# One decode step of attention with a gated MLP: wq loaded as 16 rows and then 112 rows, with x between them on SyncE's queue

## The chip, the cores and the metric

The kernel runs on one core of one Trainium2 chip. A core has a matrix engine (TensorE, PE in the profile), VectorE (DVE), ScalarE (ACT), GpSimd (POOL) and SyncE (SP). Data come from the chip's main memory by DMA, into an on-chip memory of 128 partitions. The profile counts 16 DMA engines for the core. SyncE and ScalarE each have a DMA queue of their own here, q1 and q10 in the profile.

The metric is the device time of one execution in microseconds. The kernel before takes 678.52 us, the median of three runs (678.5 to 678.8).

## The reference

Eight sequences (B = 8) each bring one new token of width D = 512. x is normalized once, and two branches use it:

```python
xn = layernorm(x)                       # 8 x 512
q  = xn @ wq                            # 512 x 4096: 32 query heads of 128
# 8 key/value heads, each shared by 4 query heads, 4096 cached positions
scores = einsum("bhqd,bhkd->bhqk", q, k) * 128 ** -0.5
o  = einsum("bhqk,bhkd->bhqd", softmax(scores), v)
s  = o.reshape(8, 4096) @ wo            # 4096 x 512

z  = gelu(xn @ w_in)                    # 512 x 1792, two halves of 896
z2 = layernorm(z[..., 896:])
m  = (z[..., :896] * (w_sp * z2 + b_sp)) @ w_out    # 896 x 512
out = x + s * silu(m)
```

All values are float32. The key and value caches are 134 MB each, so that nearly all of the traffic is the two caches, read once.

## The kernel before, in words

**Memory.** Three buffers, slots A, B and C, each have 128 partitions of 16384 floats (64 KB a partition, 8.39 MB in all). Every large load fills a slot or a part of one, always all 128 partitions, with one contiguous row of main memory for each partition. Slot B first holds wq, slot C first holds the MLP's weights (w_in and w_out, 43 KB a partition), and slot A the first half of head 0's keys. Afterwards the slots go round: for each of the 8 key/value heads the keys come as two halves (four sequences each) into A and B, and the values as two halves into C and B. For the last head the values go into A and B, while wo fills C in seven pieces that get smaller.

**Order of the work.** `Recorder` collects every operation in the order in which the program names it, works out which operation must wait for which (by the regions that they read and write) and then emits one stream of instructions for each engine. Nothing is reordered. A load with a `key` shares the semaphore of its slot; a load without one has a semaphore of its own. The heads' part of TensorE's stream runs as a loop of seven rounds, with the last head written out behind it.

**SyncE's queue.** All large loads are issued by SyncE in program order: wq (line 338), w_mlp (line 341), then keys (line 547) and values (line 553) head by head, and wo (line 558). SyncE waits before a load only until TensorE has finished with what the slot held. The first three loads wait for nothing. The fourth, the second half of head 0's keys into slot B, waits until the Q projection has read wq.

**The start.** x, with two scalars of the MLP appended to each row (8 rows of 576 floats, 18 KB), is loaded in two column halves of 288 by ScalarE (lines 334 and 335). VectorE takes its statistics (lines 387 and 388), GpSimd the power -0.5 (line 390), VectorE normalizes (line 391), and TensorE transposes (line 394) into xnT (line 395). x itself is also spread for the residual at the end (lines 402 to 406). `project_q` (lines 415 to 423) then multiplies xnT by wq from slot B in two halves, `mlp` (from line 431) uses slot C, and the heads follow: scores (line 506), softmax, values (lines 538 to 544).

**The end.** The last pieces of wo are multiplied as they land (line 574), and the result is multiplied by the gate, added to x (lines 630 and 631) and stored (line 632).

Of the kernel before, what the change touches and what calls it, by code (L numbers as in the profile page):

```python
# [16 lines left out]
B, D = 8, 512  # L17
# [13 lines left out]
WO_EARLY = 12  # L31
WO_LATE = [(WO_EARLY, 20), (20, 25), (25, 28), (28, 30), (30, 31), (31, 32)]
FOLDED = 24
FOLD_AT = 29
LOOPED = HKV - 1
X_PARTS = 2
ALIGN = 512
XW = D + 64
E = 2
# [280 lines left out]
def gqa_gmlp_decode(real, x, kT, v, wq, wo, w_mlp, out):  # L320
    nc = Recorder(real)

    def sb(name, shape, **kw):
        return real.alloc_sbuf_tensor(name, shape, F32, **kw).ap()
# [4 lines left out]
    slots = {n: sb(f"slot_{n}", [P, SLOT], align_bytes=ALIGN) for n in "ABC"}  # L329
# [1 line left out]
    tbuf = sb("tbuf", [P, B * J * G * REP])  # L331

    xs_sb = pbuf[:B, :XW]
    for c in range(0, XW, XW // X_PARTS):
        nc.scalar.dma_start(xs_sb[:, c:c + XW // X_PARTS], x[:, c:c + XW // X_PARTS])
    x_sb = xs_sb[:, :D]

    nc.sync.dma_start(slots["B"], wq, key="B")
    wq_sb = slots["B"].rearrange("p (k n) -> p k n", k=NK)
    n_in, n_mlp = NK * 2 * FH, NK * 2 * FH + NB * D  # L340
    nc.sync.dma_start(slots["C"][:, :n_mlp], w_mlp, key="C")
# [28 lines left out]
    nc.vector.tensor_copy(same8[:, (E - 1) * B:E * B], same[:, 0, :B])  # L370
    oT_end = sb("oT_end", [P, HKV * REP - FOLDED, (E - 1) * B + R])
    nc.gpsimd.memset(oT_end, 0.0)

    def shift(t, i):
        lo = (E - 1 - i) * B
        return t[:, lo:lo + R]
# [114 lines left out]
    w, wl = sb("w", [P, 1]), sb("wl", [P, 1])  # L491
    oT = sb("oT", [P, FOLDED // REP, REP, B])
    o_all = [sb(f"o_all{i}", [P, G, DH]) for i in range(2)]
# [49 lines left out]
    def combine(b):  # L543
        nc.tensor.matmul(po[:, b * REP:(b + 1) * REP], o_sb[b % 2], fold, start=True, stop=True)  # L544
# [18 lines left out]
    def folded_wo(lo, hi):  # L563
        for m in range(lo, hi):
            h, r = divmod(m, REP)
            nc.tensor.matmul(part[R * r:R * r + B, :], oT[:, h, r, :], wo_sb[:, m, :],
                             start=(m < REP), stop=(m >= FOLDED - REP))

    def direct_wo(lo, hi):
        for m in range(lo, hi):  # L570
            for i in range(E):
                for g in range(G):
                    at = g * P + i * W
                    nc.tensor.matmul(acc[R * g:R * (g + 1), :], shift(oT_end[:, m - FOLDED], i),  # L574
                                     wo_sb[:, m, at:at + W], start=(m == FOLDED and i == 0),
                                     stop=(m == HKV * REP - 1 and i == E - 1))

    def head(h):
# [21 lines left out]
        combine(B - 1)  # L600
        if h < FOLDED // REP:
            to = oT[:, h]
# [17 lines left out]
    nc.vector.tensor_copy(part_sb, part)  # L620
    direct_wo(FOLDED, FOLD_AT)
    for i in range(E):
        for g in range(G):
            lo = g * P + i * W
            nc.tensor.matmul(acc[R * g:R * (g + 1), :], shift(same8, i), part_sb[:, lo:lo + W],
                             start=False, stop=False)
    direct_wo(FOLD_AT, HKV * REP)

# [36 lines left out]
```

## Time and profile before

| | us |
|---|---|
| median of three runs | 678.52 |
| the profiled execution | 678.71 |
| its span, first to last instruction | 677.3 |
| TensorE busy with matmuls | 375.2 |
| VectorE busy | 167.5 |
| ScalarE busy | 13.4 |
| GpSimd busy | 2.8 |

The span is what the profile's views divide up; the execution's own time is 1.4 us longer. The program moved 290.90 MB, which is 429 GB/s over the span. The profile writes a load's duration in two ways: as the short time in which the issuing engine was occupied with issuing it ("SPq" for SyncE's queue, "ACTq" for ScalarE's), and as the time from the issue to its landing, which includes the loads in front of it. In a view by stretches of time a packet is put down, with its whole duration and all its bytes, at its start, so that in stretches of a microsecond the share of the DMA engines can be over 1 or 0 while they are always busy. A packet here is one partition's row of a load, or the short write at the end that reports the load as landed.

### The profile page before, as it was taken

What the parts mean: (1) busy time and instruction counts of PE and PEld (TensorE: products, weight loads), DVE (VectorE), ACT (ScalarE), POOL (GpSimd) and SP (SyncE); (2) the same over time, 40 slices, a digit from 0 to 9 for tenths busy, and PEclk for the clock granted to TensorE, in tenths of its full rate; (3) what the DMA queues carried; (4) which work ended last, traced back from release to release, by engine and by line L of the source; (5) the groups of instructions that cost most, each with busy time, mean ns of one, the idle gap of its engine ahead of it and who ended that gap; (6) DMA issues with size and microseconds to landing.
All of it is one profiled execution on the core that took longest, in us unless ns stands there. A gap on an engine that the chain in (4) does not pass through costs nothing. (4 is left out here: it accounts for less than half of the span.)

```text
span 677.3 us, 5857 instructions
## 1 busy us (share of the span) xinstructions
PE 375.2 (55%) x2658; PEld 119.5 (18%) x2658; DVE 167.5 (25%) x277; ACT 13.4 (2%) x27; POOL 2.8 (0%) x14
## 2 busy tenths in 40 slices
PE   0547554546665455456755454655654465655657
PEld 0122121112111111111211121211211121111212
DVE  2141042302430033401521024401432024400342
ACT  0000000000000000000000000000000000000000
POOL 1000000000000000000000000000000000000000
PEclk9967666878767678877766678887676678766697
DMA  8999999999999999999999999999999999999997
GB/s 373 449 434 434 433 434 433 434 433 433 433 433 433 433 433 433 434 433 433 433 433 433 433 434 433 433 433 437 437 437 437 433 437 445 433 437 434 404 423 318
DMA packets 6233, 290.90 MB, mean 429 GB/s; under 512 B 832, under 2 KB 848, under 8 KB 1360
## 3 DMA queue, kind: packets, MB, share of 16 engines
q1 hardware_dynamic: 6192, 290.75, 99.3%
q8 instruction: 7, 0.11, 0.1%
q10 hardware_dynamic: 32, 0.02, 0.0%
q14 instruction: 2, 0.02, 0.0%
HBM read 290.74 MB, written 0.03 MB: 429 GB/s over the span
## 5 line engine op out<-in xcount | busy, mean ns | idle before, releaser
L506 PE MATMUL sc<-slot_B,qz 128*32 128x512 f32 x512 | 74.4, 746 | 76.6 <-PEq L506 76.6
L538 PE MATMUL o_ps<-slot_B,tbuf 128*16 128x512 f32 x512 | 77.5, 732 | 70.5 <-PEq L538 61.6
L506 PE MATMUL sc<-slot_A,qz 128*32 128x512 f32 x512 | 74.4, 746 | 47.6 <-PEq L506 47.6
L540 DVE TENSOR_TENSOR o_all<-o_ps,diag 128x512 f32<-128x512 f32 x64 | 44.3, 691 | 161.0 <-PE o_ps L538 161.0
L538 PE MATMUL o_ps<-slot_C,tbuf 128*16 128x512 f32 x448 | 67.0, 739 | 20.5 <-PEq L538 20.5
L510 DVE TENSOR_REDUCE nm<-sc 128x1 f32<-128x1024 f32 x8 | 9.8, 1224 | 269.5 <-PE sc L506 269.5
L541 DVE TENSOR_REDUCE o_sb<-o_all 128x128 f32<-128x512 f32 x64 | 67.8, 1060 | 2.2
L506 PEld LDWEIGHTS sc<-slot_B,qz 128*32 128x32 f32 x512 | 20.4, 134 | 130.5 <-issue 130.5
L506 PEld LDWEIGHTS sc<-slot_A,qz 128*32 128x32 f32 x512 | 20.7, 133 | 94.8 <-issue 94.8
L544 PE MATMUL po<-fold,o_sb 128*128 128x4 f32 x128 | 25.6, 270 | 12.3 <-PEq L544 12.3
L544 PEld LDWEIGHTS po<-fold,o_sb 128*128 128x128 f32 x128 | 20.3, 199 | 68.5 <-issue 64.2
L538 PEld LDWEIGHTS o_ps<-slot_B,tbuf 128*16 128x16 f32 x512 | 13.4, 106 | 100.5 <-issue 90.2
L538 PEld LDWEIGHTS o_ps<-slot_C,tbuf 128*16 128x16 f32 x448 | 13.7, 112 | 57.0 <-issue 56.8
L528 PE MATMUL scr<-ident,pbuf 128*128 128x128 f32 x64 | 14.8, 409 | 10.6 <-PEq L528 9.3
L511 ACT ACTIVATE pbuf<-sc,nm 128x1024 f32<-128x1024 f32 x8 | 8.9, 1114 | 556.1 <-DVE nm L510 556.1
L528 PEld LDWEIGHTS scr<-ident,pbuf 128*128 128x128 f32 x64 | 11.8, 211 | 11.0 <-issue 9.7
L529 DVE COPY tbuf<-scr 128x512 f32<-128x512 f32 x16 | 11.1, 692 | 10.6 <-PE scr L528 10.6
L415 PE MATMUL scr<-slot_B,xnT 128*32 128x512 f32 x64 | 9.0, 713 | 8.2 <-PEq L415 8.2
L538 PE MATMUL o_ps<-slot_A,tbuf 128*16 128x512 f32 x64 | 9.8, 753 | 3.9 <-PEq L538 3.9
L514 PE MATMUL scr<-ident,nm 128*1 128x128 f32 x8 | 2.2, 269 | 11.8 <-PEq L514 10.4
L394 PE MATMUL scr<-ident,tbuf 8*128 8x8 f32 x4 | 0.6, 255 | 12.9 <-DVE tbuf L391 12.9
L521 PE MATMUL scr<-wl,same 128*128 128x1 f32 x16 | 3.5, 286 | 6.1 <-PEq L521 5.4
(102 smaller groups left out, 88.4 us busy)
## 6 DMA issues: line engine op xcount, KB each, us to landing
slot_B<-in_v SPq DMA_DIRECT2D x2, 4096.0 KB, 33.8
slot_C<-in_w_mlp SPq DMA_DIRECT2D x1, 5376.0 KB, 34.2
slot_C<-in_wo SPq DMA_DIRECT2D x1, 3072.0 KB, 35.4
slot_C<-in_wo SPq DMA_DIRECT2D x1, 2048.0 KB, 41.4
slot_C<-in_wo SPq DMA_DIRECT2D x1, 1280.0 KB, 44.0
slot_C<-in_wo SPq DMA_DIRECT2D x1, 768.0 KB, 45.4
slot_C<-in_wo SPq DMA_DIRECT2D x1, 512.0 KB, 46.1
slot_C<-in_wo SPq DMA_DIRECT2D x2, 256.0 KB, 46.4
```

What stands on the lines that cost most here:

```text
L415: nc.tensor.matmul(pq[R * g:R * (g + 1), :], xnT[:, k, :], wq_sb[:, k, lo:lo + REP * DH], start=(k == 0), stop=(k == NK - 1))
L506: nc.tensor.matmul(sc[R * g:R * (g + 1), c, :], qz[:, b * R:(b + 1) * R], k_sb[:, i, c, g, :], start=(b == 0), stop=(b == B - 1))
L510: nc.vector.tensor_reduce(nm, sc, op=ALU.max, axis=AX.XY, negate=True)
L511: nc.scalar.activation(p.rearrange("p j s -> p (j s)"), sc.rearrange("p c s -> p (c s)"), AF.Exp, bias=nm, accum_out=l)
L514: nc.tensor.transpose(a, nm, ident)
L521: nc.tensor.matmul(tot, same_all, wl, start=True, stop=True)
L528: nc.tensor.transpose(t[:, j * P:(j + 1) * P], p[:, 4 * c + j, :], ident)
L529: nc.vector.tensor_copy(pT[:, :, 4 * c:4 * c + 4].rearrange("p b j (g r) -> p (j g) b r", g=G), t.rearrange("p (m b r) -> p m b r", b=B, r ...
L538: nc.tensor.matmul(of[R * c:R * c + G * REP, :], pT[:, b, j, :], v_unit[:, j], start=(j < G), stop=(j >= J - G))
L540: nc.vector.tensor_mul(o_all[b % 2], o, diag[:, :, None].to_broadcast([P, G, DH]))
L541: nc.vector.tensor_reduce(o_sb[b % 2], o_all[b % 2].rearrange("p g d -> p d g"), op=ALU.add, axis=AX.X)
L544: nc.tensor.matmul(po[:, b * REP:(b + 1) * REP], o_sb[b % 2], fold, start=True, stop=True)
```

## The change

wq's load is split by rows: partitions 0 to 15 first, then partitions 16 to 127. x is no longer loaded by ScalarE in two halves; SyncE issues it in one transfer between the two parts of wq. The two parts of wq have semaphores of their own, where the whole load had that of slot B, so that the first multiplication with wq waits for both. All other operations are the same and stand in the same order; behind this place their lines are lower by one.

```diff
 FOLDED = 24
+FIRST = 16
 FOLD_AT = 29
 LOOPED = HKV - 1
-X_PARTS = 2
...
     xs_sb = pbuf[:B, :XW]
-    for c in range(0, XW, XW // X_PARTS):
-        nc.scalar.dma_start(xs_sb[:, c:c + XW // X_PARTS], x[:, c:c + XW // X_PARTS])
     x_sb = xs_sb[:, :D]
-
-    nc.sync.dma_start(slots["B"], wq, key="B")
+    nc.sync.dma_start(slots["B"][:FIRST], wq[:FIRST])
+    nc.sync.dma_start(xs_sb, x)
+    nc.sync.dma_start(slots["B"][FIRST:], wq[FIRST:])
     wq_sb = slots["B"].rearrange("p (k n) -> p k n", k=NK)
```

## The prediction

> **What bounds the kernel now.** I read the page's span, slices and queues first, then its chain that ended last, then the start of the timeline and of the DMA traffic, because the change touches only the first three loads.
>
> ```profile
> span 677.3 us, 5857 instructions
> ...
> DMA  8999999999999999999999999999999999999997
> GB/s 373 449 434 434 433 434 433 434 433 433 433 433 433 433 433 433 434 433 433 433 433 433 433 434 433 433 433 437 437 437 437 433 437 445 433 437 434 404 423 318
> ...
> q1 hardware_dynamic: 6192, 290.75, 99.3%
> ...
> q10 hardware_dynamic: 32, 0.02, 0.0%
> ...
> DMA 7%; PE 1%; SPq 0%; DVE 0%; issue 0%
> ```
>
> The transfers are busy in every slice at 433 to 437 GB/s, and SP's queue (q1) takes 99.3% of sixteen engines' span. q10 is ScalarE's queue, which carries only x. The chain is short, and most of it is one wait for a load:
>
> ```profile
> 616.62 8.87 PE sc L506 x64
> ...
> 628.26 46.46 DMA slot_C<-in_wo
> 674.72 0.04 issue
> ```
>
> That load is the last of a queue that never ran dry. Busy time over three stretches (the last two columns are the share of the sixteen DMA engines and GB/s):
>
> ```profile
> 0.00:1.60 1.60, 0.00 (x0) 0.00 (x0) 0.09 (x1) 0.00 (x0) 0.83 (x9) 1.00 0.00 0
> ...
> 40.00:660.00 620.00, 346.54 (x2315) 108.02 (x2308) 155.81 (x242) 12.15 (x26) 0.57 (x1) 0.74 1.00 433
> ```
>
> Nothing moves for 1.6 us, and then the engines are full: share 1.00 at 433 GB/s for 620 us. So the time is the start, plus bytes over rate, plus a tail of some 2.6 us after the last load lands at 674.72. TensorE is busy 346.54 of those 620 us and waits for data. **Whatever the slowest DMA engine loses in the first 40 us is carried to the end**, because later there is no idle DMA time to take it back.
>
> The one place where it could be regained is a stretch in which the queue waits for SP to issue. The page's DMA issues show there is none:
>
> ```profile
> slot_B<-in_kT SPq DMA_DIRECT2D x8, 27.9
> ...
> slot_B<-in_v SPq DMA_DIRECT2D x7, 29.1
> ...
> slot_B<-in_wq SPq DMA_DIRECT2D x1, 21.9
> ```
>
> An 8.39 MB transfer takes 8.39/433 = 19.4 us. The ones into slot B, the latest issued, land 27.9 and 29.1 us after issue, so 8.5 to 9.7 us of other traffic is still ahead of them. A late start shifts their issue as much as their landing, and the margin stays.
>
> **The change part by part.** The start of the kernel:
>
> ```profile
> 0.73 0.90 ACTq L335 DMA_DIRECT2D pbuf<-in_x  x2
> 0.74 0.38 SPq L338 DMA_DIRECT2D slot_B<-in_wq  x1
> 1.16 0.42 SPq L341 DMA_DIRECT2D slot_C<-in_w_mlp  x1
> 1.64 0.42 SPq L547 DMA_DIRECT2D slot_A<-in_kT  x1
> 1.66 1.28 ACT L445 ACT_TABLE_LOAD   x1 [1.66 <-PEq L657]
> 10.55 0.68 DVE L387 BATCH_NORM_STATS2 st<-pbuf 8x6 f32<-8x512 f32 x1 [6.89 <-DMA pbuf<-in_x]
> 13.50 0.19 DVE L395 COPY xnT<-scr 128x32 f32<-128x32 f32 x1 [0.69 <-PE scr L394]
> 22.80 5.35 PE L415 MATMUL scr<-slot_B,xnT 128*32 128x512 f32 x32 [8.25 <-PEq L415]
> 33.25 0.33 SPq L547 DMA_DIRECT2D slot_B<-in_kT  x1
> 43.87 0.63 ACT L445 ACTIVATE pbuf<-pbuf 128x512 f32<-128x512 f32 x1 [40.93 <-DVE pbuf L444]
> ```
>
> *ScalarE's two issues go* (0.90 us). ScalarE's table load can start at about 0.75 instead of 1.66, but its first real work is at 43.87: worth 0. If that cover were gone, it would be worth 0.9 us.
>
> *SP issues three loads where it issued one.* At the 0.38 to 0.42 us of the rows above plus 0.04 between issues, w_mlp and the first K move 2 x 0.46 = 0.9 us later. The engines don't notice: the first 16 rows are 1.05 MB, which is 2.4 us at 433 GB/s, and the third issue is over at about 0.74 + 3 x 0.46 = 2.1 us, before those rows can be through. Cost 0; without that cover up to 0.9 us.
>
> *x lands at another time.* It now stands behind sixteen rows of wq in the same queue. The statistics start at 10.55 and the transposed x is ready at 13.69, so the layernorm needs 3.1 us; its user, the first Q projection, starts at 22.80, when wq has landed. In the changed order x stands ahead of 112 rows, which need at least 112 x 65.5 KB / 433 GB/s = 16.9 us, so x is ready well before wq whatever the sixteen rows cost. Worth 0 either way. That earlier or later layernorm is the visible effect, but not one on the path.
>
> *The projection waits for two loads instead of one.* That is one more wait on TensorE's queue before line 415, which was idle for 8.25 us there: 0.04 us (the "issue" pieces of the chain), hidden because K for slot B is issued with 8.5 us in hand.
>
> *Packets.* Two x transfers of 8 rows with 8 end packets each are the 32 of q10. One x transfer has 16, and one more wq transfer adds 16 end packets: 32 again. 0.
>
> *The two wq transfers themselves.* This is the term that matters. The traffic at the start, put down at the start of each packet:
>
> ```profile
> 1.70:1.90 0.20, 0.00 (x0) 0.00 (x0) 0.17 (x1) 0.20 (x1) 0.20 (x2) 1.00 6.21 1989
> ...
> 2.90:3.00 0.10, 0.00 (x0) 0.00 (x0) 0.10 (x1) 0.04 (x1) 0.00 (x0) 1.00 1.51 655
> ...
> 4.80:5.50 0.70, 0.00 (x0) 0.00 (x0) 0.00 (x0) 0.00 (x0) 0.00 (x0) 1.00 3.46 1498
> ...
> 7.20:7.90 0.70, 0.00 (x0) 0.00 (x0) 0.00 (x0) 0.00 (x0) 0.00 (x0) 1.00 3.49 1511
> ...
> 9.60:10.30 0.70, 0.00 (x0) 0.00 (x0) 0.00 (x0) 0.00 (x0) 0.00 (x0) 1.00 3.46 1498
> ...
> 12.10:12.70 0.60, 0.00 (x0) 0.00 (x0) 0.42 (x1) 0.00 (x0) 0.14 (x1) 1.00 4.03 1748
> ```
>
> In 4.80:5.50 start 1498 x 0.7 = 1049 KB, which is sixteen rows of 65.5 KB: every engine takes one row, and the next sixteen start 2.42 us later (4.8, 7.2, 9.6, 12.1). One engine carries one row in 2.42 us, 27.1 GB/s (2.90:3.00 holds a single row: 1.51 x 0.1 x 16 = 2.42 us). The spread of the starts stays 0.6 to 0.7 us, so in a 128-row transfer no engine gets in another's way. Every large transfer of the kernel has that form, so the trace has no large transfer to fewer partitions, and the price of one is not shown.
>
> The new first transfer lands in 16 neighbouring partitions, and all sixteen engines work there at once. Bounds: if neighbours don't share a way into the memory, one row time, 2.42 us; if all share one, 16 x 2.42 = 38.7 us. Between ends that far apart I take their geometric middle, 9.7 us, in which four rows share a way: the extra over 2.42 is **7.3 us** (0 to 36.3).
>
> [...]
>
> The 112 rows are seven for each engine. Bounds: lined up as the 128 rows are, 7 x 2.42 = 16.9 us, no extra; four to a way all the time, 7 x 9.7 = 67.8 us, 50.9 extra. They cover seven eighths of the partitions, so the nearest row is the 128-row load, which shares nothing; but sevens beginning at row 16 don't line up with a grouping by fours or eights, so neighbouring engines meet for part of the way. I take that the last engine goes at half speed for three of its seven rows: **7.3 us** (0 to 50.9).
>
> *Start.* Sixteen rows may start sooner than 128: the second rows start at 4.8 to 5.5, so the first ones counted from about 2.4 to 3.1, though the first packets are recorded from 1.7. A gain of at most 3.1 - 1.7 = 1.4 us; I take 0, since the first engines to start had no second row earlier than 4.8.
>
> Sum: 7.3 + 7.3 = 14.6 us. The profiled execution took 678.71 us (span 677.3), 0.19 above the median of 678.52; against that median, **693.1 us**, 2.1% slower.
>
> **The rivals.**
>
> *No shared way (not slower).* The sixteen rows cost one row time and the 112 seven. For it: all engines are busy in both transfers, every slice runs at the same 27.1 GB/s per engine, and the bytes are the same. Against it: the trace never has the engines side by side in one region. The time is 678.5, and 677.1 with the whole 1.4 us of the start. It decides from the point where sixteen rows pass in under 3.8 us (2.42 + 1.36, where 1.36 us is 0.2% of the time and about what a measurement of this kernel tells from no change). [...]
>
> *Only the sixteen rows pay.* The seven per engine spread so that no two engines meet. 678.5 + 7.3 = 685.8 us. For it: they cover 112 of 128 partitions; against it: seven divides into no even grouping.
>
> *The 112 rows pay in full.* If the rows are dealt in turn, so that neighbouring rows are in flight together all the time, 678.5 + 7.3 + 50.9 = 736.7 us, or anything from 702 up if the engines drift apart on the way.
>
> **How the numbers follow.** Both loads pay, in part: 0.50, own range 688 to 702. No shared way: 0.21, of which 0.03 gains more than 0.2%. Only the sixteen rows: 0.16. In full: 0.13. The likeliest is 693.1. The range runs from 677.8, to take in most of the not-slower case, to 702, which leaves out the full price (0.13), the larger gains (0.03) and the ends of the rest: about 0.8 inside. Faster 0.04 (the 0.03 and 0.01 for causes not listed), same 0.18, slower 0.78.
>
> **What would show it.** The sharpest mark is the statistics at line 386 of the changed kernel: they start when x lands, about 12.5 to 14 us if the sixteen rows take 9.7, about 6 us if they take 2.42. The second is the first Q projection (line 414): 22.8 if nothing is lost, about 30 if only the sixteen rows pay, about 37 by my sum, past 45 if the 112 rows pay more. The first slice's GB/s falls well below 373, and the later slices stay at 433. The last load of wo lands as much later than 674.72 as the projection starts later than 22.80. The prediction is wrong if x is early and the projection unmoved, or if a late projection is not found again at the end, which would mean a slack in the queue that I read as absent.

## The result and the profile after

The changed kernel takes 699.94 us (median of five runs, 698.69 to 700.33) against 678.68 for the kernel before on the same chip: a ratio of 1.031, with a 95% interval of 1.0295 to 1.0325. That is 21.3 us slower. The profiled execution of the changed kernel has a span of 698.6 us, against 677.3.

The page after, in the lines that answer to those shown of before:

```profile
span 698.6 us, 5856 instructions
...
GB/s 181 240 331 454 425 420 436 454 425 424 428 462 428 420 432 458 424 428 424 447 443 425 428 432 455 424 424 435 454 424 424 432 454 432 424 432 432 429 427 290
...
q1 hardware_dynamic: 6224, 290.77, 99.1%
...
DMA 7%; PE 1%; SPq 0%; DVE 0%; issue 0%
```

Only the first three slices have changed much: 181, 240 and 331 GB/s where there were 373, 449 and 434. The DMA engines still count as busy all the time. They carry the same bytes (290.90 MB on both pages) more slowly. By stretches (the last two columns are the share of the DMA engines and GB/s):

```profile
2.00:12.00 10.00, 0.00 (x0) 0.00 (x0) 1.50 (x8) 0.01 (x1) 0.43 (x3) 1.00 1.07 172
12.00:42.00 30.00, 1.68 (x22) 1.40 (x22) 2.01 (x7) 0.00 (x0) 0.54 (x1) 1.00 0.92 228
42.00:660.00 618.00, 341.05 (x2316) 108.63 (x2320) 148.12 (x241) 12.14 (x26) 0.57 (x1) 0.75 1.00 433
```

From 42 us on, the rate is the 433 GB/s of before. The timeline of the start shows x and wq landing (the statistics wait for x, line 414 for wq):

```profile
0.74 0.38 SPq L335 DMA_DIRECT2D slot_B<-in_wq  x1
1.18 0.36 SPq L336 DMA_DIRECT2D pbuf<-in_x  x1
...
1.58 0.32 SPq L337 DMA_DIRECT2D slot_B<-in_wq  x1
...
12.55 0.68 DVE L386 BATCH_NORM_STATS2 st<-pbuf 8x6 f32<-8x512 f32 x1 [8.89 <-DMA pbuf<-in_x]
...
44.61 5.48 PE L414 MATMUL scr<-slot_B,xnT 128*32 128x512 f32 x32 [28.07 <-issue]
```

x lands 2.0 us later than before and the first Q projection starts 21.8 us later (44.61 against 22.80). The chain that ended last is the old one, moved:

```profile
649.91 46.07 DMA slot_C<-in_wo
695.98 0.04 issue
```

The last piece of wo lands at 695.98, which is 21.3 us later than the 674.72 of before. What the start loses arrives at the end almost whole.

### The profile page after: what moved, and what is told of

It is laid out like the page before. It is cut to its first block, busy times and chain, and to the rows that moved or that the text cites. A ratio compares the mean times of both kernels' runs of the same rounds, so it can differ in the third digit from the quotient of the medians.

```text
span 698.6 us, 5856 instructions
## 1 busy us (share of the span) xinstructions
PE 372.3 (53%) x2658; PEld 119.0 (17%) x2658; DVE 167.4 (24%) x277; ACT 13.4 (2%) x27; POOL 2.8 (0%) x14
## 2 busy tenths in 40 slices
DMA packets 6233, 290.90 MB, mean 416 GB/s; under 512 B 840, under 2 KB 840, under 8 KB 1360
## 5 line engine op out<-in xcount | busy, mean ns | idle before, releaser
L505 PE MATMUL sc<-slot_A,qz 128*32 128x512 f32 x512 | 71.7, 723 | 48.4 <-PEq L505 48.4
L414 PE MATMUL scr<-slot_B,xnT 128*32 128x512 f32 x64 | 9.1, 721 | 28.1 <-issue 28.1
L527 PEld LDWEIGHTS scr<-ident,pbuf 128*128 128x128 f32 x64 | 11.8, 212 | 11.1 <-issue 9.7
L528 DVE COPY tbuf<-scr 128x512 f32<-128x512 f32 x16 | 11.1, 691 | 10.7 <-PE scr L527 10.7
L416 DVE TENSOR_SCALAR pbuf<-scr 128x512 f32<-128x512 f32 x2 | 1.4, 691 | 36.4 <-PE scr L414 36.4
```

The source lines that it names most:

```text
L414: nc.tensor.matmul(pq[R * g:R * (g + 1), :], xnT[:, k, :], wq_sb[:, k, lo:lo + REP * DH], start=(k == 0), stop=(k == NK - 1))
L416: nc.vector.tensor_scalar(q_sb, pq, float(DH) ** -0.5, None, op0=ALU.mult)
L505: nc.tensor.matmul(sc[R * g:R * (g + 1), c, :], qz[:, b * R:(b + 1) * R], k_sb[:, i, c, g, :], start=(b == 0), stop=(b == B - 1))
L527: nc.tensor.transpose(t[:, j * P:(j + 1) * P], p[:, 4 * c + j, :], ident)
L528: nc.vector.tensor_copy(pT[:, :, 4 * c:4 * c + 4].rearrange("p b j (g r) -> p (j g) b r", g=G), t.rearrange("p (m b r) -> p m b r", b=B, r ...
```

## The experiments

### Which part of the change costs the time

Three kernels do one part alone, or the same order with another cut.

*The split alone*, x left on ScalarE's queue:

```diff
+FIRST = 16
...
-    nc.sync.dma_start(slots["B"], wq, key="B")
+    nc.sync.dma_start(slots["B"][:FIRST], wq[:FIRST])
+    nc.sync.dma_start(slots["B"][FIRST:], wq[FIRST:])
```

> wq as 16 rows and then 112 rows, x left on ScalarE's queue in two halves. Theory W (engines that write neighbouring partitions at the same time share a way into the memory) and theory S (the same, but on the side of the source: engines that read neighbouring rows of main memory): the whole loss is in the split, 699 to 700 us, first Q projection at about 44.6. Rival X (the loss comes from x standing in SP's queue between the two parts, so that half of the engines start the 112 rows late): 678.5 us.

Measured: 700.2 us (699.58 to 700.63), ratio 1.0317 (1.03 to 1.0334).

*x alone*, in one transfer on SP's queue, ahead of a whole wq:

```diff
-    for c in range(0, XW, XW // X_PARTS):
-        nc.scalar.dma_start(xs_sb[:, c:c + XW // X_PARTS], x[:, c:c + XW // X_PARTS])
+    nc.sync.dma_start(xs_sb, x)
```

> x in one transfer on SP's queue, ahead of wq, which is whole again. Theories W and S: 678.5 us within 0.5, and x lands at about 4 us instead of 10.55, which is worth nothing because the first Q projection still starts at 22.8 to 23.3. Rival X: slower by several us, since x then delays half of the engines as well.

Measured: 678.98 us (678.72 to 679.27), ratio 1.0005 (0.9996 to 1.0015).

*The same order, cut by columns*: the first 2048 columns of all 128 partitions, x, the other columns (to the changed kernel):

```diff
-FIRST = 16
+FIRST = SLOT // 8
...
-    nc.sync.dma_start(slots["B"][:FIRST], wq[:FIRST])
+    nc.sync.dma_start(slots["B"][:, :FIRST], wq[:, :FIRST])
     nc.sync.dma_start(xs_sb, x)
-    nc.sync.dma_start(slots["B"][FIRST:], wq[FIRST:])
+    nc.sync.dma_start(slots["B"][:, FIRST:], wq[:, FIRST:])
```

> The order of the changed kernel (first part of wq, x, rest of wq, all on SP's queue), but wq is split by columns: 2048 of the 16384 columns for all 128 partitions, then the other 14336. Bytes of the two parts are those of the 16 and 112 rows. Theories W and S: each engine has its own partitions again, 678.5 us within 1, first Q projection at about 23, x lands at about 6 us. Rival F (a split costs by itself: the second transfer starts late, or a transfer of 1 MB runs badly): slower by more than 2 us, the projection late.

Measured: 678.62 us (678.41 to 679.02), ratio 1.0001 (0.9991 to 1.0011). The timelines, first of the split alone:

```profile
22.09 0.68 DVE L389 BATCH_NORM_STATS2 st<-pbuf 8x6 f32<-8x512 f32 x1 [18.43 <-DMA pbuf<-in_x]
44.75 6.14 PE L417 MATMUL scr<-slot_B,xnT 128*32 128x512 f32 x32 [18.66 <-issue]
```

of x alone:

```profile
3.57 0.62 DVE L386 BATCH_NORM_STATS2 st<-pbuf 8x6 f32<-8x512 f32 x1
23.36 6.29 PE L414 MATMUL scr<-slot_B,xnT 128*32 128x512 f32 x32 [15.85 <-PEq L414]
```

and of the cut by columns, where the projection's first eight multiplications start on the first part:

```profile
5.79 0.68 DVE L386 BATCH_NORM_STATS2 st<-pbuf 8x6 f32<-8x512 f32 x1 [2.13 <-DMA pbuf<-in_x]
9.72 1.94 PE L414 MATMUL scr<-slot_B,xnT 128*32 128x512 f32 x8
22.70 5.24 PE L414 MATMUL scr<-slot_B,xnT 128*32 128x512 f32 x24 [11.05 <-DMA slot_B<-in_wq]
```

The whole loss is in the split by rows. x on SP's queue costs and brings nothing that these runs can tell: the time is the same with x landing at 3.57, 5.79 or 10.55 where wq is fast, and nearly the same with 12.55 or 22.09 where wq is slow. Two loads instead of one cost nothing either where each covers all 128 partitions (ratio 1.0001). The columns also size the first term of the sum: the same 1.05 MB ahead of x, in all partitions, let x land at 5.79; in 16 partitions at 12.55. The sixteen rows cost **6.8 us** more, and of the 21.8 us of the projection **15.0** remain for the 112 rows.

### Source or destination

A kernel with twelve loads of wq's rows into slot C ahead of everything, each issued when the one before has landed. Slot C is overwritten afterwards. In this probe and those below, `Recorder` also counts the step between partitions when it works out the region of a load (two lines, left out here).

```diff
+    C = slots["C"]
+    for to, fr in [(C, wq),
+                   (C[0:16], wq[0:16]), (C[0:16], wq[0:128:8]),
+                   (C[0:128:8], wq[0:16]), (C[0:64:4], wq[0:16]), (C[0:112:7], wq[0:16]),
+                   (C[0:4], wq[0:4]), (C[0:16:4], wq[0:4]),
+                   (C[0:32], wq[0:32]), (C[0:64], wq[0:64]),
+                   (C[0:112], wq[0:112]), (C[16:128], wq[16:128])]:
+        nc.sync.dma_start(to, fr)
     nc.sync.dma_start(slots["B"], wq, key="B")
```

> Twelve loads of wq's rows into slot C ahead of everything, each issued when the one before has landed, so that each stands alone: 128 rows; 16 neighbouring rows into 16 neighbouring partitions; every eighth row into 16 neighbouring partitions; 16 neighbouring rows into every eighth partition; the same into every fourth of 64 and every seventh of 112 partitions; 4 rows into 4 neighbouring partitions; 4 rows into every fourth of 16; 32 rows; 64 rows; rows 0 to 111; rows 16 to 127. Slot C is overwritten afterwards by the MLP's weights. With f for the fixed time from issue to landing beyond the data (about 2 us, from the first): theory W, four partitions to a way: 19.4, 9.7, 9.7, 4.8 or less, 4.8 or less, 2.4 to 4.8, 9.7, 2.4, 19.4, 38.7 at most and 19.4 at least, and about 30 for each of the 112-row loads, each plus f. Theory S: 19.4, 9.7, 2.4, 9.7, 9.7, 9.7, plus f: the spread of the source decides and that of the destination doesn't.

Packets by stretches, of the second to the fifth load (each is sixteen rows, 1049 KB):

```profile
24.00:25.50 1.50, 0.00 (x0) 0.00 (x0) 0.00 (x0) 0.00 (x0) 0.00 (x0) 1.00 5.67 699
25.50:35.50 10.00, 0.00 (x0) 0.00 (x0) 0.00 (x0) 0.00 (x0) 0.00 (x0) 1.00 0.00 0
35.50:37.00 1.50, 0.00 (x0) 0.00 (x0) 0.00 (x0) 0.00 (x0) 0.00 (x0) 1.00 5.64 699
37.00:47.50 10.50, 0.00 (x0) 0.00 (x0) 0.00 (x0) 0.00 (x0) 0.00 (x0) 1.00 0.00 0
47.50:49.00 1.50, 0.00 (x0) 0.00 (x0) 0.00 (x0) 0.00 (x0) 0.00 (x0) 1.00 3.11 699
49.00:55.50 6.50, 0.00 (x0) 0.00 (x0) 0.00 (x0) 0.00 (x0) 0.00 (x0) 1.00 0.00 0
55.50:56.50 1.00, 0.00 (x0) 0.00 (x0) 0.00 (x0) 0.00 (x0) 0.00 (x0) 1.00 4.68 1049
```

Sixteen neighbouring rows and every eighth row of the source take the same into the same 16 partitions: the next load begins some 11.5 to 12 us later, both times. With the same sixteen source rows spread over every eighth partition, the next load begins 8 us later. So the destination decides, and theory S falls. Sixteen rows into every seventh partition took 4.1 to 5.1 us a row, where theory W left most of them at 2.4, which led to the next runs.

### Two halves in the kernel

```diff
-FIRST = 16
+FIRST = 64
```

> The changed kernel with wq in two equal parts by rows, 64 and 64, and x between them. The first probe had 64 rows alone at 23.0 us from start to the start of the next, against 22.5 for 128 rows: each half takes nearly as long as the whole. Theory W: wq lands about 20 us later than in one load, the projection starts at about 43 and the time is 697 to 700 us. Rival B (the loss belongs to the small first load and to sevens that line up badly; two halves with four rows for each engine run like the whole): 678.5 to 681 us.

Measured: 699.74 us (699.51 to 699.93), ratio 1.0311 (1.0293 to 1.0328); x lands at 24.00 and the projection starts at 44.20. Theory W holds: what costs isn't a small first load. Equal halves lose as much as 16 and 112.

### What a shared way is

Two kernels in the manner of the first probe, with a small load of all partitions between each two, so that SyncE's issue of that small load marks the landing. Partitions as start, number, step.

```diff
+    C = slots["C"]
+    for lo, n, step in [(0, 8, 4), (64, 8, 4), (4, 8, 4), (0, 8, 8),
+                        (0, 2, 4), (0, 2, 1), (0, 2, 32), (0, 2, 64), (4, 2, 4), (16, 2, 4),
+                        (0, 4, 4), (16, 4, 4), (64, 4, 4), (0, 4, 32),
+                        (0, 16, 7), (0, 96, 1), (0, 128, 1)]:
+        to, fr = C[lo:lo + (n - 1) * step + 1:step], wq[:n]
+        nc.sync.dma_start(to, fr)
+        nc.sync.dma_start(C[:, :128], wq[:, :128])
     nc.sync.dma_start(slots["B"], wq, key="B")
```

> Seventeen loads of wq's rows into slot C, each alone (a load of 128 rows of 512 bytes stands between each two and waits for the one before): partitions given as start, number, step: (0, 8, 4), (64, 8, 4), (4, 8, 4), (0, 8, 8), (0, 2, 4), (0, 2, 1), (0, 2, 32), (0, 2, 64), (4, 2, 4), (16, 2, 4), (0, 4, 4), (16, 4, 4), (64, 4, 4), (0, 4, 32), (0, 16, 7), (0, 96, 1), (0, 128, 1). They ask what a shared way is, since in the first probe 16 rows into every seventh partition took 4.2 to 4.7 us a row although few of these partitions are neighbours. Theory W2 (a way is a group of four partitions together with the group 32 further; only two engines on one way slow each other): in data time 2.4, 2.4, 2.4, 4.8, 2.4, 4.8, 4.8, 2.4, 2.4, 2.4, 2.4, 2.4, 2.4, 4.8, 2.4 to 4.8, 19 to 29, 19.4. Theory N (an engine is fast only on the partitions that it serves in a 128-row load, shared or not): 2.4 for (0, 8, 4), (0, 2, 4) and (0, 4, 4); 4 to 5 for (64, 8, 4), (4, 8, 4), (4, 2, 4), (16, 2, 4), (16, 4, 4), (64, 4, 4).

From issue to the issue of the mark: two rows 4 partitions apart 5.3 us, 64 apart 5.0, 1 apart 6.5, 32 apart 7.4. Eight rows 4 apart take 5.3 from partition 0, 5.1 from 64 and 5.0 from 4, so which engine serves which group made no difference (theory N falls). Eight rows 8 apart, of which two each are 32 apart, take 7.4. Theory W2, four neighbours and the four 32 further as one way, fits these: the pairs that share by it take longer, one row time (2.42 us) more where they are 32 apart and somewhat less, 1.2 to 1.5 us, for the two direct neighbours. In the first probe four rows into partitions 0 to 3 took some 8.0 us each, four rows into 0, 4, 8 and 12 only 2.8 to 3.3.

> Thirteen loads of wq's rows into slot C, each alone as in the second probe: partitions given as start, number, step: (0, 128, 1), (0, 4, 4), (0, 4, 11), (32, 16, 4), (0, 16, 4), (28, 16, 4), (11, 16, 7), (3, 16, 7), (32, 64, 1), (0, 64, 1), (0, 16, 1), (16, 112, 1), (0, 128, 1). Theory W2 as before: a way is a group of four partitions with the group 32 further, 16 ways in all. Data times: 19.4, 2.4, 4.8 (0 and 33 share), 2.4 (sixteen different ways), 4.8 (eight ways), 4.8 (one pair shares), 2.4 (sixteen different ways), 4.8 (one pair), 9.7 (rows 32 to 95: each engine has a way to itself), 19.4 (rows 0 to 63: the same number of rows, eight ways), 9.7, about 25 if only those that share are slow, and up to 33.9 if one shared way holds up all engines at each step, 19.4. Rival D (what counts is how close together the partitions are, or how many rows a load has, not which ways they reach): (32, 16, 4) as slow as (0, 16, 4), and (32, 64, 1) as slow as (0, 64, 1).

SyncE's queue of this kernel, for (32, 16, 4), (0, 16, 4), (32, 64, 1), (0, 64, 1), (0, 16, 1), (16, 112, 1) and (0, 128, 1), issue and mark:

```profile
40.40 0.57 SPq L343 DMA_DIRECT2D slot_C<-in_wq  x1
45.49 0.33 SPq L344 DMA_DIRECT2D slot_C<-in_wq  x1
47.30 0.51 SPq L343 DMA_DIRECT2D slot_C<-in_wq  x1
54.91 0.33 SPq L344 DMA_DIRECT2D slot_C<-in_wq  x1
...
82.17 0.52 SPq L343 DMA_DIRECT2D slot_C<-in_wq  x1
94.52 0.33 SPq L344 DMA_DIRECT2D slot_C<-in_wq  x1
96.47 0.50 SPq L343 DMA_DIRECT2D slot_C<-in_wq  x1
119.26 0.33 SPq L344 DMA_DIRECT2D slot_C<-in_wq  x1
121.17 0.34 SPq L343 DMA_DIRECT2D slot_C<-in_wq  x1
132.95 0.35 SPq L344 DMA_DIRECT2D slot_C<-in_wq  x1
134.84 0.33 SPq L343 DMA_DIRECT2D slot_C<-in_wq  x1
169.56 0.33 SPq L344 DMA_DIRECT2D slot_C<-in_wq  x1
171.45 0.33 SPq L343 DMA_DIRECT2D slot_C<-in_wq  x1
193.34 0.33 SPq L344 DMA_DIRECT2D slot_C<-in_wq  x1
```

The 128 rows take 21.9 us, 2.5 more than 19.4 of data at the full rate. Less that 2.5:

| partitions | ways reached, by W2 | data time, us | at the full rate |
|---|---|---|---|
| every fourth of 32 to 92 (16 rows) | 16 | 2.6 | 2.4 |
| every fourth of 0 to 60 (16 rows) | 8 | 5.1 | 2.4 |
| 0 to 15 (16 rows) | 4 | 9.3 | 2.4 |
| 32 to 95 (64 rows) | 16 | 9.8 | 9.7 |
| 0 to 63 (64 rows) | 8 | 20.3 | 9.7 |
| 16 to 127 (112 rows) | all | 32.2 | 16.9 |

Loads of the same size, number of rows and spacing differ by a factor of two, by where they start. Rival D falls. The 1.05 MB into partitions 0 to 15 in 9.3 us are 113 GB/s without the fixed 2.5 us, and 89 with them.

*The same in the kernel*: rows 32 to 95, x, rows 0 to 31, rows 96 to 127.

```diff
-FIRST = 16
...
-    nc.sync.dma_start(slots["B"][:FIRST], wq[:FIRST])
+    nc.sync.dma_start(slots["B"][32:96], wq[32:96])
     nc.sync.dma_start(xs_sb, x)
-    nc.sync.dma_start(slots["B"][FIRST:], wq[FIRST:])
+    nc.sync.dma_start(slots["B"][:32], wq[:32])
+    nc.sync.dma_start(slots["B"][96:], wq[96:])
```

> The changed kernel with wq in three parts by rows: rows 32 to 95, then x, then rows 0 to 31, then rows 96 to 127. Theory W2: 9.7 us for the first 64 rows (sixteen ways), 9.7 for each of the others (32 rows on eight ways, two engines to a way) in place of 4.8 each: 29.1 instead of 19.4, so 9.7 us slower than before, 688 us, x lands at about 13, the first Q projection starts at about 32.5. Rival D: like the halves 0 to 63 and 64 to 127, about 699 to 700 us, or more with the smaller parts.

Measured: 689.6 us (689.38 to 689.88), ratio 1.0163 (1.0145 to 1.0181). Three parts lose half of what two halves lose, 11.0 us against 9.7 worked out ahead; the projection:

```profile
33.89 5.14 PE L414 MATMUL scr<-slot_B,xnT 128*32 128x512 f32 x32 [16.30 <-DMA slot_B<-in_wq]
```

### Why the 112 rows cost twice what was forecast

The 112 rows took 32.2 us alone, 4.6 us a row, although by the ways only a few engines can meet at any time.

```diff
+    C = slots["C"]
+    for lo, n, step in [(0, 128, 1), (32, 64, 1), (0, 96, 1), (28, 64, 1)]:
+        to, fr = C[lo:lo + (n - 1) * step + 1:step], wq[:n]
+        nc.sync.dma_start(to, fr)
+        if n == 64 and lo == 28:
+            nc.sync.dma_start(slots["A"][32:96], wq[:64])
+        nc.sync.dma_start(C[:, :128], wq[:, :128])
```

> Loads of wq's rows into slot C, each alone: 128 rows; rows to partitions 32 to 95; to partitions 0 to 95; to partitions 28 to 91, and behind this last one at once a load into partitions 32 to 95 of slot A. In 28 to 91, with four neighbouring rows for each engine, engine 0 (28 to 31) and engine 8 (60 to 63) share a way for all four rows, and the other fourteen engines have one each. The question is why the 112 rows took some 32 us. Theory L (only engines that share are slow): the fourteen start a row every 2.42 us, and begin the load into slot A 9.7 us after the start, while two go at 4.84; the load lands after 19.4. Theory H (one shared way holds up all engines that work on the load): all sixteen start a row only every 4.8 us. For 0 to 95 (six rows for each engine, of which some pair shares at each step) theory L gives 24 us, theory H 6 x 4.84 = 29.0.

In 28 to 91, fourteen engines started a row every 2.42 us and two took 4.3 to 4.8 us for each of their first two rows, so theory L held there, as it would with four neighbouring rows to each engine. It did not hold to the end of that load: when the other engines had gone on to slot A, one of them (partitions 60 to 63, if these are dealt in fours too) came onto the way of the pair by W2, three engines then took some 7 to 8 us a row, three row times, and the other thirteen 3.0 instead of 2.42. And 0 to 95 took 32.1 us from issue to mark, 29.6 of data, which is theory H: all sixteen rows of a step, from the second on, lasted 4.7 to 5.1 us. Neither holds for both. The next two kernels load a pattern three times in a row, so that each engine keeps its partition:

```diff
+    for lo, n, step in [(0, 128, 1), (11, 16, 7), (28, 16, 4), (3, 16, 7), (0, 4, 11), (0, 16, 7),
+                        (0, 16, 6)]:
+        for t in "ABC":
+            nc.sync.dma_start(slots[t][lo:lo + (n - 1) * step + 1:step], wq[:n])
+        for t in "ABC":
+            nc.sync.dma_start(slots[t][:, :128], wq[:, :128])
```

> Seven patterns of partitions, each loaded three times in a row without a wait (into slots A, B and C), so that each engine carries three rows to the same partitions, and each pattern alone: (0, 128, 1), (11, 16, 7), (28, 16, 4), (3, 16, 7), (0, 4, 11), (0, 16, 7), (0, 16, 6). By the ways of the earlier runs the pairs of engines that share are: none, none, 0 with 8, 3 with 8, 0 with 3, two pairs (0 with 5, 4 with 9), and three (1 with 6, 3 with 8, 5 with 10). The last is what 96 rows would be at their first step if each engine took six neighbouring rows. Theory L (only engines that share are slow): in every pattern the engines outside a pair start their three rows 2.42 us apart and the pairs theirs 4.84 apart. Theory H2 (a shared way also holds up engines outside the pair, for some pairs): in the pattern 28 they go on at 2.42 as in the fourth probe, in 0 with 3, 0 with 5 and the three pairs all engines of the load start 4 to 5 us apart. Theory M (96 and 112 rows are not dealt to the engines as six and seven neighbours): as theory L here, also for step 6.

Packets by stretches for (28, 16, 4), with one pair of engines on one way, from the second row on:

```profile
76.00:77.25 1.25, 0.00 (x0) 0.00 (x0) 0.00 (x0) 0.00 (x0) 0.00 (x0) 1.00 1.72 734
77.25:77.90 0.65, 0.00 (x0) 0.00 (x0) 0.00 (x0) 0.00 (x0) 0.00 (x0) 1.00 0.00 0
77.90:78.50 0.60, 0.00 (x0) 0.00 (x0) 0.00 (x0) 0.00 (x0) 0.00 (x0) 1.00 1.07 218
78.50:79.75 1.25, 0.00 (x0) 0.00 (x0) 0.00 (x0) 0.00 (x0) 0.00 (x0) 1.00 1.70 734
```

734 x 1.25 is fourteen rows, 2.5 us after that fourteen more, and 218 x 0.60 is the two rows of the pair between them, each 1.07 x 0.60 x 16 / 2 = 5.1 us long. And for (0, 16, 7), with two pairs:

```profile
129.00:131.00 2.00, 0.00 (x0) 0.00 (x0) 0.00 (x0) 0.00 (x0) 0.00 (x0) 1.00 2.47 524
131.00:134.00 3.00, 0.00 (x0) 0.00 (x0) 0.00 (x0) 0.00 (x0) 0.00 (x0) 1.00 0.00 0
134.00:136.00 2.00, 0.00 (x0) 0.00 (x0) 0.00 (x0) 0.00 (x0) 0.00 (x0) 1.00 2.49 524
```

524 x 2.00 is all sixteen rows, each 2.47 x 2.00 x 16 / 16 = 4.9 us long, and the next sixteen start 5 us later. By W2 twelve of these engines share their way with nobody, and they are held up all the same. With one pair (3 with 8, and 0 with 3) the others went on at 2.43; with three pairs all took 5.1 from the second row on. Which of number and place decides was still open.

```diff
-    for lo, n, step in [(0, 128, 1), (11, 16, 7), (28, 16, 4), (3, 16, 7), (0, 4, 11), (0, 16, 7),
-                        (0, 16, 6)]:
+    for lo, n, step in [(0, 128, 1), (36, 16, 4), (24, 16, 4), (40, 16, 4), (24, 16, 5), (1, 16, 7),
+                        (19, 16, 5)]:
```

> As the fifth probe, with other patterns: (0, 128, 1); (36, 16, 4), one pair of engines on one way in the upper half of the partitions (7 with 15); (24, 16, 4), two pairs in the lower half (0 with 8, 1 with 9); (40, 16, 4), two pairs in the upper half; (24, 16, 5), one pair in each half (0 with 7, 8 with 15); (1, 16, 7), one pair in each half (1 with 6, 9 with 14); (19, 16, 5), two pairs in the lower half (0 with 6, 1 with 8). Theory C (the number of shared ways decides: with two or more all sixteen engines are held up): only the first pattern with a pair has fourteen free engines at 2.42 us a row, in the other five all engines start rows 4.9 to 5.1 us apart. Theory P (it depends on which engines share, as 0 with 8 but not 0 with 5 leaves the others free): the patterns in which the two engines are eight apart, (36, 16, 4), (24, 16, 4) and (40, 16, 4), leave the others free, the rest do not.

With one pair, (36, 16, 4), the other fourteen ran at 2.43 us a row. In all five patterns with two pairs, in one half or in both, eight engines apart or not, all sixteen rows of a step took 4.9 to 5.2 us from the second row on. For (24, 16, 5), one pair in each half, two steps of sixteen rows, 5.0 us apart:

```profile
120.70:123.20 2.50, 0.00 (x0) 0.00 (x0) 0.00 (x0) 0.00 (x0) 0.00 (x0) 1.00 1.98 419
123.20:125.70 2.50, 0.00 (x0) 0.00 (x0) 0.00 (x0) 0.00 (x0) 0.00 (x0) 1.00 0.00 0
125.70:128.10 2.40, 0.00 (x0) 0.00 (x0) 0.00 (x0) 0.00 (x0) 0.00 (x0) 1.00 2.07 437
```

Theory C holds for the patterns tried, and theory P falls. If each engine takes seven neighbouring rows, the 112 rows have two pairs on shared ways at five of the seven steps and one pair at the third and the fourth: 5 x 5.0 us, and 2 x 2.42 to 2 x 4.84 for the others, is 30 to 35 us, around the measured 32.2.

The changed kernel's own trace has these steps. First the load of sixteen rows, then the second to the seventh step of the 112; sixteen rows start in each of these stretches, so that share times width is the mean time of a row:

```profile
1.60:2.60 1.00, 0.00 (x0) 0.00 (x0) 0.89 (x7) 0.41 (x1) 0.83 (x5) 1.00 8.45 1049
...
15.40:16.40 1.00, 1.00 (x19) 0.83 (x18) 0.19 (x1) 0.00 (x0) 0.00 (x0) 1.00 4.69 1049
20.10:21.10 1.00, 0.00 (x0) 0.00 (x0) 0.00 (x0) 0.00 (x0) 0.00 (x0) 1.00 3.19 1049
23.30:25.90 2.60, 0.00 (x0) 0.00 (x0) 0.00 (x0) 0.00 (x0) 0.00 (x0) 1.00 1.51 403
27.30:29.40 2.10, 0.00 (x0) 0.00 (x0) 0.00 (x0) 0.00 (x0) 0.00 (x0) 1.00 2.14 499
31.50:34.10 2.60, 0.00 (x0) 0.00 (x0) 0.00 (x0) 0.00 (x0) 0.00 (x0) 1.00 1.84 403
36.30:38.80 2.50, 0.00 (x0) 0.00 (x0) 0.00 (x0) 0.00 (x0) 0.00 (x0) 1.00 1.83 419
```

The sixteen rows took 8.5 us, and the six steps 4.7, 3.2, 3.9, 4.5, 4.8 and 4.6, behind a first one of some 5.2 with x's rows among it. The two quicker ones are the third and the fourth. For partitions 0 to 111 the same dealing has its steps with one pair fourth and fifth, and in the first probe these are the quick ones (3.5 and 3.6 us against 4.2 to 4.8). So the dealing in sevens fits both loads step by step. The engines outside the only pair didn't go at 2.43 here, though, but at some 3.0 and 3.9. They are out of step by then: fourteen begin their fourth rows at 23.3 to 23.8, the last two only after 25.2, by the dealing those of the third step's pair, so that pairs of different steps are at work together. That this is what holds up the others there isn't shown.

## Why the prediction was right, point by point, and where a term was too small

- **The bound, and that the start is carried to the end**: right. The projection starts 21.8 us later and the last load lands 21.3 later; the rate from 42 us on is 433 GB/s as before, and the keys into slot B land 28.1 us after issue instead of 27.9, so that the margin stayed too.
- **The edits costed at nothing** (ScalarE's issues, SP's two more issues, x's landing, the second wait, the packets): right. x alone makes no difference (1.0005, 0.9996 to 1.0015), the cut by columns has two loads, x between them and two waits, and makes none either (1.0001). ScalarE's table load starts at 0.73 and w_mlp is issued 0.78 us later, as worked out within 0.15 us.
- **The sixteen rows, +7.3**: right in mechanism and size. They cost 6.8 in the kernel and 6.9 alone (9.3 against 2.4). The chosen middle, four rows to a way, fits what the runs showed (9.3 us is 3.8 row times of 2.42). That it hit so well is partly luck: it is the geometric middle of 2.42 and 38.7, and no row of the trace of before spoke for four rows to a way rather than two or eight.
- **The 112 rows, +7.3**: the step that failed in size. "The last engine goes at half speed for three of its seven rows" took each engine for itself. The rows cost 15.0 in the kernel and 15.3 alone (32.2 against 16.9), because at a step with two shared ways the engines that share nothing by W2 were held up too, and five of the seven rows took 4.5 to 5.2 us instead of 2.42. With 15.0 in its place the sum is 678.5 + 6.8 + 15.0 = 700.3, against 699.94 measured. The prediction's marks say the same: x lands at 12.55, as named for sixteen rows in 9.7 us, and the projection at 44.61 is near the "past 45" named for 112 rows that pay more, not near the 37 of the sum.
- **The start, 0**: nothing was gained there. The first packets of the sixteen rows start where those of the 128 did (1.75 to 1.80 us, against 1.70 to 1.75).
- **The rivals**: "no shared way" would have been right for a cut by columns (1.0001), or for rows 32 to 95 (9.8 us alone). "Only the sixteen rows pay" and "the 112 rows pay in full" (50.9) are both refuted by the 32.2 us. The sum had 14.6 us where 21.3 were measured. The range of 677.8 to 702 held the result through the likeliest case's own upper end, not through its middle.

## What to carry to other kernels

In this kernel, bound by DMA at 433 GB/s, cutting one load of 8.39 MB by partitions cost 21 us: time the parts alone before such a cut, as the probes do, and try a cut by columns if a part must come early, so that each part still covers all 128 partitions. In this kernel nearly every microsecond that a slow transfer lost at the start was paid at the end: 21.8 and 21.3 in the changed kernel, 11.1 and 11.0 with three parts. The part that came early was worth nothing here, by columns either (ratio 1.0001). When a disturbance touches a few engines of a load, ask whether the others can go on without them before counting only the few.

## What was not expected

- In the probes, two rows on one way slow only themselves when they are the only pair (2.43 us a row for the others), but two such pairs slow all sixteen engines to 4.9 to 5.2 us a row. Why the second pair does this stays open, and so does why three rows on one way slowed the others a little (3.0).
- 64 rows into partitions 32 to 95 run at the full rate (9.8 us), and 64 rows into 0 to 63 at half of it (20.3).
- In the kernel before, the small transfer of x on another queue went in step with whole rows of the large one. The packets of the second half start at 7.2 us, as the engines' second rows of wq end, and the writes that report it come at 9.7 to 10.1, as the third rows end; the statistics start at 10.55. Beside the slowed rows of the split alone they start at 22.09.
